# Attention into a hard-swish MLP on one core: a new order and a new sharing of engines, with score tiles as single steps

## The chip, the core and the metric

The kernel runs on one core of a Trainium2 chip. A core has a matrix engine, TensorE (PE in the profile, its weight loads PEld), VectorE (DVE), ScalarE (ACT), GpSimd (POOL) and SyncE (SP), which here only issues DMAs. Each engine takes its instructions in the order in which the program gives them. The metric is the device time of one execution in microseconds (us), the median of three runs.

## The reference

Eight batches of twelve heads with 448 rows of 64 go through attention, and the result through a two-layer MLP whose middle is a hard swish:

```python
q_n, k_n = rmsnorm(q, g_q), rmsnorm(k, g_k)        # x / sqrt(mean(x*x) + 1e-6) * g
scores = 1/sqrt(64) * q_n @ k_n.T                  # per batch and head, 448 x 448
attn = exp(scores - max); attn = attn / (sum + 1e-9)
x = (attn @ v), heads side by side                 # 3584 x 768
h = x @ w_in                                       # 768 x 2048
g = h * clip(h + 3, 0, 6) / 6
out = g @ w_out                                    # 2048 x 768
```

All inputs and the output are fp32.

## The kernel before, in words

Two heads make a pair P, 0 to 47; six pairs make a batch b. The 448 rows of a head are cut into four tiles t of 112. The functions of the kernel do not emit instructions at once. Each calls `plan.add` with the engines that could do the step (`ways`), what it reads and writes, and a function that emits it. A step's number is its place among these calls. The table `WAY` then picks for a step another of its ways than the first, and the list `ORDER` gives the order in which all steps are emitted; since each engine works through its own steps in that order, the list is the program's schedule. The costs, due times, `load` and `since` in the calls served the search that wrote the two tables. They emit nothing.

The stages of a pair are these, with their lines in the profile:

- `load`: q, k and v of the pair by SP (L388), three DMAs of 256 KB each. The rings hold five pairs, so a load waits until the pair five before it has been used.
- `prep`: squares of q and k, on ACT (L401) or POOL (L403); sums over 64 on DVE (L410); the inverse root by Ln and Exp on ACT (L415, L418); the scaling of q and k on POOL (L427; pair 0 on DVE); and the cast of v to bf16 with a column of ones, `va`, on POOL (L351), ACT (L347) or DVE (L345).
- `trans`: q and k turned, into T. Pairs 0 to 12 by PE (L479) with a copy of each half on DVE (L349, L490) or ACT (L347, L488), the k half times the gains. Pairs 13 on by a transposing DMA on SP (L455), and then a scaling of the k half on DVE or ACT (L464). Pairs 8 to 12 turn in the first bank of the two score buffers S. The ring of T holds four pairs.
- `score`: two matmuls for each tile, one for each head, on half the rows of PE each (L510), and an exp on ACT (L519). A tile goes into one of two score buffers S, taken in turn, or, late in the kernel, into X. For pairs 0 to 5 a step is one tile, for 6 to 23 it is two, and for 24 on it is three, two and three tiles for each two pairs. A step of several tiles is emitted as a whole and writes all its buffers.
- `av`: eight matmuls for each tile (L531), summed in the one buffer X over the pair's four tiles.
- `finish`: reciprocal and product on DVE (L547, L550), giving xn; then turned into xT, by PE with a copy for batches 0 and 1 (L566, copies L349 and L347), by a transposing DMA on SP after that (L557).

The MLP takes a batch once its six xT are there. `h_group` b.f makes 128 of the 2048 columns of h for a batch: six matmuls (L587) into one of two buffers M, Relu on ACT (L594) and min and product on DVE (L597). `y_group` takes two batches at a time and 128 rows: twice 16 matmuls of 384 columns (L618), a copy on ACT or DVE and DMAs out (L639). The weights come as four slices of w_in and four of w_out, 768 KB in SBUF each (1.57 MB in fp32), by POOL's DMA queue (L653, L658); h group f needs slice f // 4, and the part p of a y group needs slice p of w_out.

Where PE would idle at the beginning, it runs matmuls on zeros (L356, L536).

Of the kernel before, what the change touches and what calls it, by code (L numbers as in the profile page):

```python
# [14 lines left out]
EXP = mybir.ActivationFunctionType.Exp  # L15
# [6 lines left out]
WAY = {53: 1, 63: 2, 67: 1, 68: 1, 69: 1, 78: 1, 83: 1, 84: 1, 95: 1, 101: 1, 126: 1, 132: 2, 157: 1,  # L22
# [10 lines left out]


class Plan:

# [12 lines left out]
    def add(self, ways, want, fn, reads=(), writes=(), load=(), since=0.0, soon=()):  # L49
        i = len(self.ops)  # L50
        self.way[i] = WAY.get(i, 0)
        eng, occ, fin = ways[self.way[i]]
        soon = dict(soon)
        preds = {}

        def after(p, lat):
            preds[p] = max(preds.get(p, 0.0), lat)

        for r in reads:
            if r in self.last:  # L60
                after(*self.last[r])
            self.readers.setdefault(r, []).append((i, fin))
        for w in writes:
            for p in self.readers.get(w, ()):
                if p[0] != i:
                    after(*p)
            if w in self.last:
                after(*self.last[w])
        for w in writes:
            self.last[w] = (i, soon.get(w, fin))  # L70
            self.readers[w] = []
        self.ops.append((eng, occ, fin, want, fn, preds, load, since))
        self.ways.append(ways)
        return i

    def emit(self, order):

        place = {i: n for n, i in enumerate(order)}
        assert len(place) == len(self.ops)
        for i, o in enumerate(self.ops):  # L80
            assert all(place[p] < place[i] for p in o[5])
        for i in order:
            self.ops[i][4](self.ops[i][0])
# [124 lines left out]
def kernel(  # L208
# [17 lines left out]
    T = 4  # L226
# [110 lines left out]
    def pool(n, rate):  # L337
        return POOL, 0.02 + n * rate, 0.05 + n * rate
# [443 lines left out]
```

## Time and profile before

| | us |
|---|---|
| median of 3 runs | 430.36 (429.74 to 430.75) |
| span of the profiled execution | 427.8 |
| PE busy | 415.1 (97%) |
| ACT busy | 296.7 (69%) |
| DVE busy | 219.6 (51%) |
| POOL busy | 171.1 (40%) |
| first exp / last exp of pair 5 starts | 11.53 / 38.24 |
| first h matmul (L587) | 38.14 |
| first y matmul (L618) | 71.78 |
| last matmul ends | 424.4 |

For the profiled execution no time of its own is given beside its span; the median of the timed runs lies 2.56 us above that span. Shares of busy time are means over a beginning, in which attention for the first batch and the DMAs are all there is to do, and a long middle in which attention and MLP go side by side. So the profile is read by stretches of time. The granted TensorE clock is 1.00 in every stretch.

### The profile page before, as it was taken

The page shows a single profiled execution, that of the slowest core. Times are in us where ns is not written, and L with a number is a line of the kernel's source. Part 1 is how long each engine was busy: PE and PEld are TensorE (multiplying, and loading weights), DVE is VectorE, ACT ScalarE, POOL GpSimd, SP SyncE. Part 2 cuts the span into 40 slices and gives each one's busy share as a digit, 9 for nine tenths or more (in the row PEclk, how much of TensorE's full clock was granted, in tenths as well). Part 3 has the DMA queues.
Part 4 walks back from the last instruction along what each step waited for, and adds up shares of the span by engine and source line. Part 5 has one row for each costly group of instructions (what it writes and reads, how often), then busy time and mean ns, then how long its engine had stood idle before and what let it go on. Part 6 is the DMA issues. An engine that isn't in the chain of part 4 may idle for free.

```text
span 427.8 us, 9914 instructions
## 1 busy us (share of the span) xinstructions
PE 415.1 (97%) x3946; PEld 238.6 (56%) x3946; DVE 219.6 (51%) x405; ACT 296.7 (69%) x535; POOL 171.1 (40%) x188
## 2 busy tenths in 40 slices
PE   9678999999999999999999999999999999999996
PEld 8455455555555555555555555555555555655554
DVE  5665776547787965665545454434434332243211
ACT  5999898889998988968757977575575556222221
POOL 2899865874767866255524340312200000000000
PEclk9999999999999999999999999999999999999999
DMA  8999999698799999668565865352413221021113
GB/s 258 349 249 288 242 240 250 149 267 231 197 237 262 229 234 227 187 155 233 136 170 132 215 156 124 75 125 55 93 33 70 50 60 49 11 75 37 38 38 113
DMA packets 98931, 67.77 MB, mean 158 GB/s; under 512 B 53156, under 2 KB 95428, under 8 KB 98884
## 3 DMA queue, kind: packets, MB, share of 16 engines
q1 hardware_dynamic: 93248, 60.50, 54.5%
q0 software_dynamic: 5248, 6.29, 8.4%
q8 instruction: 31, 0.51, 0.5%
q10 hardware_dynamic: 388, 0.34, 0.3%
q14 instruction: 16, 0.13, 0.1%
HBM read 50.23 MB, written 11.01 MB: 143 GB/s over the span
## 4 chain that ended last, share of the span: by engine, by line
PE 90%; ACT 4%; issue 2%; DVE 1%; DMA 1%; POOL 1%; SPq 0%; POOLq 0%
PE M L587 32%; PE M L618 29%; PE X L531 10%; PE S L510 8%; PE S L618 5%; ACT eT L519 2%; PE X L587 1%; DMA qk<-in_k_dram 1%; PE S L587 1%; PE X L510 1%; PE X L618 1%; POOL qks L427 1%; DVE gT L597 0%; SPq L388 0%; ACT ts L594 0%
## 5 line engine op out<-in xcount | busy, mean ns | idle before, releaser
L519 ACT ACTIVATE eT<-S 112x896 bf16<-112x896 f32 x168 | 148.1, 918 | 13.8 <-PE S L510 13.3
L587 PE MATMUL M<-xT,w_in_sb 128*128 128x448 bf16 x714 | 153.2, 353 | 0.8 <-ACT xT L347 0.4
L618 PE MATMUL M<-w_out_sb,gT 128*128 128x384 bf16 x752 | 135.9, 326 | 0.0
L597 DVE SCALAR_TENSOR_TENSOR gT<-ts,M 128x448 bf16<-128x448 f32 x119 | 73.4, 619 | 101.9 <-ACT ts L594 101.7
L427 POOL TENSOR_TENSOR qks<-qk,rs 112x512 bf16<-112x512 f32 x94 | 96.2, 1043 | 65.5 <-DMA T<-qks 31.9
L618 PEld LDWEIGHTS <-gT 128*128 128x128 bf16 x912 | 84.8, 98 | 61.9 <-issue 9.7
L594 ACT ACTIVATE ts<-M 128x448 f32<-128x448 f32 x119 | 64.8, 548 | 61.0 <-PE M L587 59.8
L587 PEld LDWEIGHTS <-w_in_sb 128*128 128x128 bf16 x768 | 69.9, 98 | 65.7 <-issue 10.9
L403 POOL TENSOR_TENSOR sq<-qk 112x512 f32<-112x512 f32 x56 | 57.7, 1041 | 43.4 <-DMA qk<-in_k_dram 18.2
L531 PEld LDWEIGHTS <-eT 112*128 112x128 bf16 x1536 | 57.1, 97 | 18.1 <-issue 8.2
L410 DVE TENSOR_REDUCE ssq<-sq 112x16 f32<-112x1024 f32 (+1 forms) x50 | 57.9, 1172 | 15.8 <-ACT sq L401 11.9
L531 PE MATMUL X<-va,eT 112*128 112x65 bf16 x1536 | 62.3, 194 | 1.0 <-DVE xT L349 0.8
L510 PE MATMUL S<-T 64*128 64x448 bf16 x336 | 47.3, 354 | 2.1 <-ACT eT L519 1.5
L550 DVE TENSOR_TENSOR xn<-X,rd 112x512 bf16<-112x512 f32 x48 | 33.2, 691 | 1.6
L351 POOL CAST va<-vf 112x512 bf16<-112x512 f32 x20 | 12.3, 613 | 41.1 <-PE X L531 38.8
L510 PEld LDWEIGHTS <-T 64*128 64x128 bf16 x384 | 12.8, 94 | 27.9 <-issue 21.0
L401 ACT ACTIVATE sq<-qk 112x512 f32<-112x512 f32 x40 | 24.9, 629 | 4.7 <-DMA qk<-in_q_dram 2.3
L347 ACT COPY y<-M 128x384 f32<-128x384 f32 x26 | 12.5, 481 | 18.4 <-PE M L618 18.1
L547 DVE RECIPROCAL rd<-X 112x8 f32<-112x8 f32 x48 | 9.8, 204 | 28.1 <-PE X L531 27.9
L349 DVE COPY y<-M 128x384 f32<-128x384 f32 x21 | 11.7, 555 | 22.8 <-PE M L618 22.6
L519 ACT ACTIVATE eT<-X 112x896 bf16<-112x896 f32 x24 | 22.1, 923 | 0.0
L618 PE MATMUL S<-w_out_sb,gT 128*128 128x384 bf16 (+1 forms) x128 | 21.8, 316 | 0.0
(58 smaller groups left out, 188.3 us busy)
## 6 DMA issues: line engine op xcount, KB each, us to landing
qk<-in_q_dram SPq DMA_DIRECT2D x47, 256.0 KB, 4.2
qk<-in_k_dram SPq DMA_DIRECT2D x47, 256.0 KB, 4.0
vf<-in_v_dram SPq DMA_DIRECT2D x47, 256.0 KB, 4.8
w_in_sb<-in_moe_w_in_dram POOLq DMA_DIRECT2D x4, 768.0 KB, 12.7
w_out_sb<-in_moe_w_out_dram POOLq DMA_DIRECT2D x4, 768.0 KB, 14.5
out_dram<-y SPq DMA_DIRECT2D x7, 336.0 KB, 2.8
out_dram<-y SPq DMA_DIRECT2D x8, 288.0 KB, 2.7
out_dram<-y SPq DMA_DIRECT2D x8, 240.0 KB, 3.4
```

Source lines behind the costliest of these rows:

```text
L401: em(nc.scalar.square(out=sq[:, i], in_=x))
L403: em(nc.gpsimd.tensor_tensor(out=sq[:, i], in0=x, in1=x, op=A_MULT))
L410: em(nc.vector.tensor_reduce(out=ssq[:, s].rearrange("p i n -> p (i n)"), in_=sq[:, s].rearrange("p i (n d) -> p (i n) d", d=D), axis=AX_X ...
L427: em((nc.vector if e == DVE else nc.gpsimd).tensor_tensor(out=qks[:, i].rearrange("p t h d -> p h t d"), in0=qk[:, i].rearrange("p h (t d) ...
L510: em(nc.tensor.matmul(out=ps[:, a, 0:S], lhsT=qkT[r, S + t * TP:S + t * TP + 128], rhs=qkT[r, 0:S], start=True, stop=True))
L519: em(nc.scalar.activation(out=eT[:, t, 0:S2].rearrange("p (a s) -> p a s", a=2), in_=ps[0:TP, :, 0:S], func=EXP, bias=0.0, scale=1.0))
L531: em(nc.tensor.matmul(out=X_ps[:, a, i * E1:(i + 1) * E1], lhsT=eT[:, t, c:c + 128], rhs=va[:, a, t, :], start=(t == 0 and i == 0), stop=( ...
L550: em(nc.vector.tensor_tensor(out=xn[:].rearrange("p i a d -> p a i d"), in0=xv[:, :, :, 0:D], in1=rd[:].unsqueeze(3).to_broadcast([TP, 2, ...
L587: em(nc.tensor.matmul(out=ps[:, 0:S], lhsT=w_in_sb[:, kt, f * 128:(f + 1) * 128], rhs=xT[:, kt, :], start=(kt == 0), stop=(kt == NKT - 1)))
L594: em(nc.scalar.activation(out=ts[:], in_=ps[:, 0:S], func=RELU, bias=0.5, scale=1.0 / 6.0))
L597: em(nc.vector.scalar_tensor_tensor(out=gT[:, f, e * S:(e + 1) * S], in0=ts[:], scalar=1.0, in1=ps[:, 0:S], op0=A_MIN, op1=A_MULT))
L618: em(nc.tensor.matmul(out=ps[:, 0:nc0], lhsT=gT[:, f, i * 128:(i + 1) * 128], rhs=w_out_sb[:, f, c0:c0 + nc0], start=(f == 0), stop=(f == ...
```

## The change

The score steps of several tiles are gone: `score` makes one step for each tile. This adds 96 steps, so all numbers behind the first of them shift, and both tables are written anew, by a search over four copies of a model with durations stretched at random. The figures of that model were changed as well (`load`, `since`, some durations, the fields of a step); none of these emits an instruction. No instruction's shape or amount of data is changed.

What the new tables say, counted per engine:

| | before | after |
|---|---|---|
| squares on ACT / POOL | 40 / 56 | 44 / 52 |
| casts of v on ACT / POOL / DVE | 12 / 20 / 16 | 8 / 24 / 16 |
| copies of T (PE's transposes) on ACT / DVE | 10 / 16 | 4 / 22 |
| scalings of T's k half on ACT / DVE | 16 / 19 | 15 / 20 |
| copies of xT on ACT / DVE | 4 / 8 | 2 / 10 |
| copies of y on ACT / DVE | 32 / 25 | 30 / 27 |
| order of the weights on POOL's queue (i: w_in, o: w_out) | i1 i0 o2 i2 i3 o1 o0 o3 | i0 i1 i2 o0 i3 o1 o2 o3 |
| first loads on SP's queue (pair and tensor) | 0q 0k 2q 1v 1k 1q 3v 0v | 0q 0k 1q 2q 2k 1k 3q 3k |

ACT's queue from the first exp to pair 5's last one, in short (E pair.tile: exp; sq: square; n: Ln and Exp of a norm, named where the second of the two stands; cT, cX, va: copies and the cast):

```
before: E0.1 E0.0 E0.3 n2 sq3.k E0.2 E1.1 va2 E1.0 E1.3 E1.2 n3 sq5.k E2.1 E2.0 sq4.q E2.3 E2.2 sq6.q n4 E3.0 E3.1 n5
        E3.2 E3.3 n6 cX2 E4.1 E4.0 E4.3 sq8.q cT6.q E5.1 E4.2 n7 E5.3 cT6.k E5.0 cX4 E5.2
after:  E0.0 E0.1 E0.2 E0.3 sq4.q E1.0 n3 E1.1 n4 E1.2 E1.3 sq6.q n5 sq6.k E2.0 E2.1 E2.2 n6 sq7.q E2.3 E3.0 E3.1 E3.2
        E3.3 E4.0 E4.1 n7 E4.2 E4.3 E5.0 n8 E5.1 E5.2 E5.3
```

The diff, without most of the two tables:

```diff
-WAY = {53: 1, 63: 2, 67: 1, 68: 1, 69: 1, 78: 1, 83: 1, 84: 1, 95: 1, 101: 1, 126: 1, 132: 2, 157: 1,
...
+WAY = {
+    63: 2, 65: 1, 68: 1, 69: 1, 78: 2, 84: 1, 90: 1, 94: 1, 95: 1, 101: 2, 126: 1, 132: 2, 163: 1, 218: 1,
...
-    def add(self, ways, want, fn, reads=(), writes=(), load=(), since=0.0, soon=()):
+    def add(self, ways, want, fn, reads=(), writes=(), load=(), since=0.0, half=False):
...
 ORDER = [
-    8, 9, 20, 13, 21, 22, 15, 23, 11, 24, 28, 10, 25, 19, 29, 53, 26, 12, 30, 27, 14, 54, 31, 16, 55, 32, 33,
...
-            plan.add([(SP, 0.5, 2.5)], want, fn, writes=res, load=(0.84, 60))
+            plan.add([(SP, 0.5, 2.5)], want, fn, writes=res, load=(0.745,))
...
-            plan.add([(SP, 0.6, 2.5)], want, f_d, reads, [(tn, i) for i in range(2)],
-                     load=(1.7, 30))
+            plan.add([(SP, 1.22, 2.5)], want, f_d, reads, [(tn, i) for i in range(2)],
+                     load=(1.25,))
...
-    def score(slots, want):
-        parts = [(P, t, *((X_ps, ("X",)) if wide else sbank())) for P, t, wide in slots]
+    def score(P, t, wide, want):
+        ps, res = (X_ps, ("X",)) if wide else sbank()
+        qkT, eT, n = T_r[P % NT], eT_r[P % NE], P % NE
 
         def f_s(_):
-            for P, t, ps, _ in parts:
-                qkT = T_r[P % NT]
-                for a in range(2):
-                    r = slice(a * 64, a * 64 + 64)
-                    em(nc.tensor.matmul(
-                        out=ps[:, a, 0:S], lhsT=qkT[r, S + t * TP:S + t * TP + 128], rhs=qkT[r, 0:S],
-                        start=True, stop=True))
...
-        plan.add(pe(0.2 + 0.19 * len(parts)), want, f_s, sorted(reads), [p[3] for p in parts], soon=soon)
...
+            for a in range(2):
+                r = slice(a * 64, a * 64 + 64)
+                em(nc.tensor.matmul(
+                    out=ps[:, a, 0:S], lhsT=qkT[r, S + t * TP:S + t * TP + 128], rhs=qkT[r, 0:S],
+                    start=True, stop=True))
...
+        plan.add(pe(0.196), want, f_s, [(("T", P % NT), i) for i in range(2)], [res], half=True)
+        plan.add([act(S2)], want, f_e, [res], [("e", n, t)])
...
-            plan.add([(POOL, 0.8, 3.0)], -20.0, f_i, [], [("w_in", c)], load=(4.56, 95), since=AT_IN[c])
+            plan.add([(POOL, 0.8, 3.0)], -20.0, f_i, [], [("w_in", c)], load=(4.0,), since=AT_IN[c])
...
-            score(slots, gw)
+            for slot in slots:
+                score(*slot, gw)
```

More of the change, by code (lines that the diff above doesn't have):

```diff
@@ L21 @@
 PE, ACT, DVE, POOL, SP = "PE", "ACT", "DVE", "POOL", "SP"
-WAY = {53: 1, 63: 2, 67: 1, 68: 1, 69: 1, 78: 1, 83: 1, 84: 1, 95: 1, 101: 1, 126: 1, 132: 2, 157: 1,
[10 rows of a table removed]
+WAY = {
[11 rows of a table added]
+}
 class Plan:
@@ L52, in add @@
         eng, occ, fin = ways[self.way[i]]
[L53 to L57, printed above, removed]
+        preds = set()
         for r in reads:
             if r in self.last:
-                after(*self.last[r])
-            self.readers.setdefault(r, []).append((i, fin))
+                preds.add(self.last[r])
+            self.readers.setdefault(r, []).append(i)
         for w in writes:
-            for p in self.readers.get(w, ()):
-                if p[0] != i:
-                    after(*p)
+            preds.update(p for p in self.readers.get(w, ()) if p != i)
             if w in self.last:
-                after(*self.last[w])
+                preds.add(self.last[w])
         for w in writes:
-            self.last[w] = (i, soon.get(w, fin))
+            self.last[w] = i
             self.readers[w] = []
-        self.ops.append((eng, occ, fin, want, fn, preds, load, since))
+        self.ops.append((eng, occ, fin, want, fn, preds, load, since, half))
         self.ways.append(ways)
@@ L371, in f_gp @@
             em(nc.vector.tensor_copy(out=gp_t[:], in_=X_ps[:, 0, 0:1]))
-        plan.add([(DVE, 0.15, 0.25)], want, f_g8, [], [("g8",)], since=2.5)
+        plan.add([(DVE, 0.15, 0.25)], want, f_g8, [], [("g8",)], since=3.4)
         plan.add(pe(0.3), want, f_gm, [("g8",)], [("X",)])
@@ L431, in f_sc @@
                     op=A_MULT))
-            plan.add([(DVE, 0.75, 0.85) if P == 0 else pool(n, 1.95e-3)], want + 0.01, f_sc,
+            plan.add([(DVE, 1.0, 1.1) if P == 0 else pool(n, 1.95e-3)], want + 0.01, f_sc,
                      [("qk", P % NQK, i), ("rs", P % NRS, i)], [("qks", P % NQS, i)])
@@ L437, in prep @@
         ways = [(POOL, 0.57, 0.62), act(n, 0.03)][::-1 if P in V_ACT else 1]
-        plan.add(ways + [(DVE, 0.62, 0.7)], want + 2.0, f_v,
+        plan.add(ways + [(DVE, 0.7, 0.8)], want + 2.0, f_v,
                  [("vf", P % NV)], [("va", P % NVA)])
@@ L466, in f_kt @@
                     em(nc.vector.tensor_scalar(x, x, gp_t[:], None, A_MULT, A_ADD, accum_out=junk_t[:]))
-            plan.add([(DVE, 0.62, 0.7), act(S, 0.1)], want + 3.0, f_kt, [("gp",)], [(tn, 1)])
+            plan.add([(DVE, 0.7, 0.8), act(S, 0.1)], want + 3.0, f_kt, [("gp",)], [(tn, 1)])
             return
@@ L500, in sbank, with f_e @@
         return S_r[u], ("S", u)
-    def score(slots, want):
-        parts = [(P, t, *((X_ps, ("X",)) if wide else sbank())) for P, t, wide in slots]
+    def score(P, t, wide, want):
+        ps, res = (X_ps, ("X",)) if wide else sbank()
+        qkT, eT, n = T_r[P % NT], eT_r[P % NE], P % NE
         def f_s(_):
-            for P, t, ps, _ in parts:
-                qkT = T_r[P % NT]
-                for a in range(2):
-                    r = slice(a * 64, a * 64 + 64)
-                    em(nc.tensor.matmul(
-                        out=ps[:, a, 0:S], lhsT=qkT[r, S + t * TP:S + t * TP + 128], rhs=qkT[r, 0:S],
-                        start=True, stop=True))
-        soon = [(p[3], 0.1 + 0.19 * (n + 1) + MM_FIN) for n, p in enumerate(parts)]
-        reads = {(("T", p[0] % NT), i) for p in parts for i in range(2)}
-        plan.add(pe(0.2 + 0.19 * len(parts)), want, f_s, sorted(reads), [p[3] for p in parts], soon=soon)
-        for P, t, ps, res in parts:
-            eT, n = eT_r[P % NE], P % NE
-            def f_e(_, t=t, ps=ps, eT=eT):
-                em(nc.scalar.activation(
-                    out=eT[:, t, 0:S2].rearrange("p (a s) -> p a s", a=2),
-                    in_=ps[0:TP, :, 0:S], func=EXP, bias=0.0, scale=1.0))
-            plan.add([act(S2)], want, f_e, [res], [("e", n, t)])
+            for a in range(2):
[3 more added lines that the diff above has]
+                    start=True, stop=True))
+        def f_e(_):
+            em(nc.scalar.activation(
+                out=eT[:, t, 0:S2].rearrange("p (a s) -> p a s", a=2),
+                in_=ps[0:TP, :, 0:S], func=EXP, bias=0.0, scale=1.0))
+        plan.add(pe(0.196), want, f_s, [(("T", P % NT), i) for i in range(2)], [res], half=True)
+        plan.add([act(S2)], want, f_e, [res], [("e", n, t)])
     def av(P, t, want):
@@ L538, in f_av @@
                     skip_group_check=True))
-        plan.add(pe(0.238), want, f_av, [("e", P % NE, t), ("va", P % NVA)], [("X",)])
+        plan.add(pe(0.246), want, f_av, [("e", P % NE, t), ("va", P % NVA)], [("X",)])
     def finish(P, want):
@@ L559, in f_d @@
                     in_=xn[:].rearrange("p i a d -> p (i a d)")))
-            plan.add([(SP, 0.6, 2.5)], want, f_d, [("xn", P % NXN)], [("xT", b % NXT, j)], load=(0.85, 30))
+            plan.add([(SP, 1.22, 2.5)], want, f_d, [("xn", P % NXN)], [("xT", b % NXT, j)], load=(0.62,))
             return
@@ L589, in f_h @@
                         rhs=xT[:, kt, :], start=(kt == 0), stop=(kt == NKT - 1)))
-            plan.add(pe(0.189 * len(kts)), want + part * dt * 2 / np, f_h,
+            plan.add(pe(0.1897 * len(kts)), want + part * dt * 2 / np, f_h,
                      [("xT", b % NXT, kt) for kt in kts] + [("w_in", f // 4)], [res])
@@ L621, in f_y @@
                             start=(f == 0), stop=(f == NFT - 1)))
-                plan.add(pe(4 * (0.003 + nc0 / 2400)), want + (n * 4 + part) * dt, f_y,
+                plan.add(pe(4 * (0.0033 + nc0 / 2400)), want + (n * 4 + part) * dt, f_y,
                          [("g", g % 2, e, f) for e in es for f in range(part * 4, part * 4 + 4)]
@@ L643, in y_group @@
                 else:
-                    plan.add([(SP, 0.4, 2.4)], want + 8 * dt, f_o,
+                    plan.add([(SP, 0.52, 2.4)], want + 8 * dt, f_o,
                              [("y", yk, n)] if final else [("y", yk, i) for i in range(3)], [],
-                             load=(m * nc0 * 1.4e-5, 110))
+                             load=(m * nc0 * 1.4e-5,))
                 c += m
@@ L660, in f_o @@
                     in_=moe_w_out[c * 512:(c + 1) * 512, :].rearrange("(f p) n -> p f n", p=128)))
-            plan.add([(POOL, 0.8, 3.0)], -20.0, f_o, [], [("w_out", c)], load=(4.8, 150), since=AT_OUT[c])
+            plan.add([(POOL, 0.8, 3.0)], -20.0, f_o, [], [("w_out", c)], load=(4.04,), since=AT_OUT[c])
     H_C, Y_C, A_C = 1.134, 5.216, 2.1
```

259 rows, old and new, of tables (ORDER, WAY) are left out of this document.

## The prediction

> **What bounds the kernel now.** I read the page's engine shares first, then the busy time by stretch, then TensorE's (PE's) waits, and last the queues of the stretch in which PE is not full. The page's busy tenths, 10.7 us to a slice:
>
> ```profile
> PE   9678999999999999999999999999999999999996
> ACT  5999898889998988968757977575575556222221
> POOL 2899865874767866255524340312200000000000
> DMA  8999999698799999668565865352413221021113
> ```
>
> The busy time by stretch (length, then busy us of each engine, granted clock, DMA share, GB/s):
>
> ```profile
> 12.00:16.00 4.00, 2.81 (x45) 1.85 (x46) 2.75 (x4) 3.83 (x8) 4.00 (x5) 1.00 1.09 350
> 25.00:30.00 5.00, 4.18 (x82) 2.76 (x79) 2.77 (x5) 4.97 (x12) 5.00 (x6) 1.00 1.17 258
> 35.00:40.00 5.00, 4.09 (x58) 2.48 (x58) 2.51 (x4) 4.60 (x11) 4.98 (x7) 1.00 1.12 301
> 50.00:55.00 5.00, 5.00 (x45) 2.69 (x44) 4.20 (x10) 4.69 (x11) 3.94 (x4) 1.00 1.17 244
> 100.00:150.00 50.00, 50.00 (x516) 26.65 (x515) 40.06 (x75) 45.37 (x85) 32.80 (x34) 1.00 0.91 228
> ```
>
> From 72 us on, the list of PE's waits is empty: PE is full, and the end is set by how much PE work is left and by when PE fills up. Before about 45 us ACT and POOL are full (4.97 and 5.00 of 5.00) and PE is not. So a new order can save time only ahead of about 72 us, and can lose it anywhere. ACT's own rows between the first exp and the last one of pair 5 (11.5 to 39.2 us; busy us, mean ns, idle before):
>
> ```profile
> L519 ACT ACTIVATE eT<-S 112x896 bf16<-112x896 f32 x24 | 21.0, 915 | 1.0 <-PE S L510 0.9
> L401 ACT ACTIVATE sq<-qk 112x512 f32<-112x512 f32 x6 | 3.8, 628 | 0.0
> L347 ACT COPY xT<-X 128x448 bf16<-128x448 bf16 x2 | 1.1, 546 | 0.0
> L488 ACT ACTIVATE T<-M,gp_t 128x448 bf16<-128x448 bf16 x1 | 0.6, 627 | 0.0
> L347 ACT CAST va<-vf 112x512 bf16<-112x512 f32 x1 | 0.6, 620 | 0.0
> L347 ACT COPY T<-M 128x448 bf16<-128x448 bf16 x1 | 0.5, 523 | 0.0
> ```
>
> Instructions overlap their neighbours by about 0.1 us (a square starts at 22.44, the next exp at 22.96), so one costs the queue its duration less 0.1. Last, PE in order of time: where it first fills up, and what a score run costs.
>
> ```profile
> 43.53 0.54 PE L587 MATMUL M<-xT,w_in_sb 128*128 128x448 bf16 x2 [0.42 <-ACT xT L347]
> 44.49 0.55 PE L510 MATMUL S<-T 64*128 64x448 bf16 x4
> ...
> 143.11 0.42 PE L531 MATMUL X<-va,eT 112*128 112x65 bf16 x8
> 143.36 1.30 PE L587 MATMUL M<-xT,w_in_sb 128*128 128x448 bf16 x6
> 144.50 0.90 PE L531 MATMUL X<-va,eT 112*128 112x65 bf16 x24
> 145.32 0.55 PE L510 MATMUL S<-T 64*128 64x448 bf16 x4
> 145.81 1.48 PE L618 MATMUL M<-w_out_sb,gT 128*128 128x384 bf16 x8
> ```
>
> An attention-times-V step (8 matmuls) takes 143.36 − 143.11 = 0.25; three ahead of a score run take 0.82 where 0.74 is due, so entering a score run costs 0.08 to 0.1. The run of two tiles then takes 0.49 start to start, where runs of three take 0.67: 0.19 a tile and 0.1 besides. One more score run is thus 0.2 us of PE.
>
> **The change, part by part.** No arithmetic is added: the counts of squares, exps, casts, copies and matmuls are equal. Moved are order and engine.
>
> (1) ACT's queue up to pair 5's last exp. Old, behind the first exp at 11.53: 24 exps, 5 squares, 6 Ln and 6 Exp of the norms, one v cast, two T copies, two xT copies; last exp over at 39.16 (38.24 + 0.92). New: 24 exps, 4 squares, the same 12 small ones, no cast, no copy. Gone: one square 0.53, one cast 0.52, xT copies 2 x 0.45, T copies 0.52 and 0.42, in all 2.9. Ahead of the first exp the new queue holds one square more and one cast less. Its chain runs: the fifth load landed at 7.78 (2.78 + 4.99) and loads land about 0.75 apart (0.256 MB at 350 GB/s), so the sixth, now pair 1's k, lands near 8.4; its square until 9.5; the sum on DVE waits for pair 2's (1.2) and takes 0.65, until 10.3; T copy 10.7; scores; first exp near 11.2, 0.35 earlier. With the same 1.4 us of gaps, pair 5's last exp ends at 39.16 − 2.9 − 0.35 = 35.9. **−3.3.** The six instructions go to DVE and POOL. DVE's summed work up to pair 5's xn grows from 25.2 to 29.2 us, with 33 us to do it in; POOL's up to pair 5's last scaling falls from 20 to 18. Neither comes to the front, so the shift itself costs nothing; without that room it would cost its 4 us.
>
> (2) Score tiles singly. In the old order pair 6's tiles 2 and 3 are one step, behind both T8 transposes (in the same banks) and behind an xT copy on ACT; it starts at 44.49, 5.3 after pair 5's last exp. By then the old PE has 21.8 us of its real work behind it. In the new order, tile 2 goes once its own bank is free. After 35.9 come a square 0.53, exp 0.84, exp 0.84, two small ones 0.25, a wait of about 0.4 for the T8 copy, then exp; PE reaches the same amount of work 4 us after pair 5's last exp. 5.3 − 4.0 = 1.3, and 0.3 more because it stands at 22.1 by then. **−1.6**
>
> (3) Score runs. Counted in the order, neighbours in PE's queue taken together: 88 runs before (8, 56 and 24 of one, two and three tiles), 93 after (17, 53, 23). 5 x 0.2 = **+1.0**, on the path since nearly all come where PE is full. If the extra ones all lay in PE's early gaps it would be 0.
>
> (4) Weights. On POOL's queue the first slice of w_in is now first of the eight, seventeenth in its queue (fourteenth before, with slice 1 in front). 12 squares and scalings at 1.0 and one cast at 0.6, started near 10.3, another cast and one wait of 1: issue near 24. PE wants it at about 33.5, ahead of pair 5's last score tile. The issues seen landed after 11.2 to 15.3: 35.2 to 39.3, a wait of 1.7 to 5.8. The lower end is none: the row nearest is slice 1 of the old kernel (issued 17.82, landed 29.0, nothing ahead of it in its queue), and eight loads went out beside it at 0.75 each; now SP waits for POOL's scalings, and about five go out between 22.5 and 31. 11.2 − 3 x 0.75 = 9.0: lands at 33. I take **+0.5**. Slice 1 now is issued at about 32 instead of 17.8 and wanted at 44 (11.2 gives 43.2: no wait; 15.3 gives 3.3); slices 2 and 3 and w_out are wanted 9 to 20 after their issue, and w_out part 3 leaves POOL at about 56 where it left at 61.9.
> [...]
>
> (5) DVE beside POOL. Pair 0's two scalings stay on DVE; they took 1.11 (beside a POOL cast) and 0.68 (alone). Now the second meets POOL's square of pair 2. Bounds 0 and +1.04 (the square); I take the rows' difference, **+0.4**, as it lies on the chain to the first exp.
> [...]
>
> (6) SP's queue. Pair 14's transpose stands at place 45 (55 before), behind it four q and k loads and one more, then pair 13's transpose, and only then pair 12's v load (52; was 36). SP is blocked until pair 14 is scaled and pair 10's scores have freed its T buffer, about 71. The v load then lands near 80 and is wanted by PE near 85; pair 13's T is there near 79 and wanted near 83. Cost 0 to 4 (each of POOL's steps ahead 15% slower); taken **0**, the cover being 4 us.
>
> (7) Later. The PE work between a tile's scores and its use by V has median 7.1 us after the change and 4.3 before, between a full bank and its next use 2.3 and 2.2, between a y group and the next use of its bank 1.6 and 1.4, the least 0.77 and 0.9. Where the old list shows no wait I take **+0.5** for shorter least gaps, between 0 and 3 (the five least gaps each 0.2 short, and one transpose 2 late). The cost figures edited in the plan emit no instruction.
>
> Sum: −3.3 − 1.6 + 1.0 + 0.5 + 0.4 + 0.5 = −2.5. The profiled span is 427.8, so 425.3 after; the median of the runs shown is 430.36, 2.56 above that span, and I carry this over: **427.9**. This case's own range is 426.4 to 429.3.
>
> **The rivals.**
> More is kept: parts 4, 5 and 7 cost nothing and the extra runs fall in gaps: −4.9 + 0.2, 425.7. For it: the freer steps of 7, and POOL's lower sum. Against: DMA's share above 1.0 all the way to 70 us.
> Late weights (the other side): w_in slice 0 takes 15.3 instead of 9, and PE stands from 33.5 to 39.3 in front of pair 5's last tile, ACT dry behind it. 5.8 − 0.5 = +5.3 on the forecast, less some 1.2 that ACT's backlog makes good: 432.0. It decides from 12.5 between issue and landing on (3.0 of wait, of which 0.5 is in the sum, eat the gain). For it: two of the three early w_in rows are at 12.1 and 15.3. Against: fewer loads beside it.
> SP's block: T13 or va12 comes 4 to 6 us late, after PE has filled up, and nothing makes it good: 432. For it: a queue in order with five loads behind a wait. Against: the covers of 4 us.
> Nothing moves: ACT's shorter queue only uncovers DMA, whose 65 us of early transfers (44 loads at 0.75, 8 slices at 4) end near 70 either way: PE fills when it did, and the runs cost 1.0, half of it in gaps: 430.9.
>
> **How the numbers follow.** Forecast 0.48; more kept 0.14; late weights 0.18; SP's block 0.12; nothing moves 0.08. Measuring cannot tell under 0.2% (0.86 us) from no change. Faster: 0.48 + 0.14 and 0.03 of the late-weights cases under 2.6 us of wait, 0.65. Same: 0.02 of late weights, 0.02 of SP's block, 0.04 of nothing moves, 0.08. Slower: the other 0.27. The range, 425.4 to 432.0, leaves out some 0.06 below (the better part of more-is-kept) and 0.14 above (the worse halves of late weights and SP's block).
>
> **What would show it.** Part 1: pair 5's last exp over near 36, DVE and POOL not full between 12 and 36. Part 2: exp of pair 6's tile 2 near 39 instead of 45, and the first L618 matmul near 68 instead of 71.78. Part 3: runs of two score matmuls in the full stretch, 0.2 dearer in all. Part 4: no wait over 1 us on w_in before an L587 matmul. Parts 6 and 7: no PE wait behind 72. I am wrong if PE stands at L587 between 33 and 50, if POOL or DMA and not ACT sets the exps, or if PE's waits behind 72 sum to over 2.

## The result and the profile after

The kernel after takes 431.84 us (median of 19, 430.27 to 435.81), the kernel before 430.62 (19, 429.50 to 432.56): a ratio of 1.0039, 95% interval 1.0020 to 1.0058. It is slower by 0.4%; 427.9 and faster was forecast. The profiled execution of after has a span of 429.5 us, 1.7 above that of before, and a time of 431.26. The h matmul is L578 now (L587 before), the y matmul L609, the score L504, V L522, the scaling L422, the square on POOL L398.

The busy tenths of the page, 10.7 us to a slice:

```profile
PE   7889998999999999999999999999999999999996
ACT  6988987779888778767877784686866564124110
POOL 2999946477754454327131523341604000000000
DMA  8899997888966998575967287724850720131015
```

Busy time by stretch (length, then busy us of PE, PEld, DVE, ACT, POOL, granted clock, DMA share, GB/s), the stretches shown of before and four more:

```profile
12.00:16.00 4.00, 3.84 (x54) 2.79 (x52) 3.06 (x8) 3.79 (x7) 4.00 (x5) 1.00 1.01 335
25.00:30.00 5.00, 4.18 (x74) 2.79 (x71) 4.12 (x10) 4.74 (x8) 4.98 (x6) 1.00 1.01 207
35.00:40.00 5.00, 5.00 (x77) 3.25 (x75) 3.63 (x7) 4.94 (x8) 4.55 (x6) 1.00 1.13 245
50.00:55.00 5.00, 5.00 (x52) 2.69 (x51) 3.32 (x8) 4.69 (x12) 4.44 (x5) 1.00 1.19 205
60.00:70.00 10.00, 9.79 (x93) 5.08 (x91) 6.44 (x14) 8.43 (x15) 2.16 (x3) 1.00 1.15 232
70.00:80.00 10.00, 9.04 (x110) 5.14 (x111) 4.41 (x8) 7.02 (x14) 7.52 (x9) 1.00 0.46 109
110.00:125.00 15.00, 14.22 (x163) 7.55 (x160) 10.70 (x22) 11.99 (x24) 10.18 (x12) 1.00 0.89 183
125.00:160.00 35.00, 34.38 (x307) 18.69 (x305) 19.20 (x34) 29.07 (x52) 15.83 (x17) 1.00 0.92 218
```

PE is full between 35 and 40 us, where it had 4.09 of 5.00. So the beginning did become shorter. But PE is short again later: by 1.2 us between 60 and 80 us, where the old one was short by 0.45, and by 1.4 between 110 and 160 us, where the old one was full. POOL has 2.16 of 10 us to do from 60 to 70. PE's waits behind 45 us, after (the tile and line that waited, who ended the wait; us in all, times, longest):

```profile
PE M L578 <- DVE gT L588: 1.0, 2, 0.7
PE X L522 <- POOL va L346: 0.6, 1, 0.6
PE M L609 <- DVE gT L588: 0.4, 1, 0.4
PE M L578 <- ACT y L342: 0.2, 1, 0.2
```

**PE's lag** makes this countable: the wall time less the PE work done by then, each step of PE's order taken at its price in the rows (a matmul of h 0.190, four matmuls of y 0.65, a step of V 0.246, four transposes 0.2, scores 0.19 a tile and 0.2 a run; the last eight steps of y have half the columns and half the price). Where PE is full the lag stands still. PE's whole work is 400.8 us before and 401.6 after. The lag in us at:

| run | 40 | 60 | 80 | 150 | 400 | span |
|---|---|---|---|---|---|---|
| before | 21.7 | 22.9 | 23.9 | 23.8 | 23.5 | 427.8 |
| after | 19.5 | 19.7 | 21.7 | 23.6 | 23.6 | 429.5 |

After was ahead by 3.2 us at 60 us. By 160 us (23.9) it had lost all of it. The list of waits above shows only 2.2 us of this: start to start, a wait costs PE some 0.17 more than its row says (at 116.48 the list has 0.71 and the lag grows by 0.88), and gaps below 0.15 us are not listed. The 1.7 of the span are 0.8 more PE work, 0.2 of lag, and 0.7 behind PE's end.

The first loss, in the timeline of SP, POOL, DVE and PE, after (start, us, what; in brackets the idle time ahead of it and who ended it):

```profile
53.61 0.93 SPq L383 DMA_DIRECT2D qk<-in_k_dram  x2
74.91 1.35 SPq L450 DMA_TRANSPOSE T<-qks  x1
76.32 0.57 SPq L383 DMA_DIRECT2D qk<-in_q_dram  x1
...
66.16 1.03 POOL L398 TENSOR_TENSOR sq<-qk 112x512 f32<-112x512 f32 x1 [7.99 <-DMA qk<-in_k_dram]
68.87 1.04 POOL L398 TENSOR_TENSOR sq<-qk 112x512 f32<-112x512 f32 x1 [1.68 <-DMA qk<-in_k_dram]
69.86 0.61 POOL L346 CAST va<-vf 112x512 bf16<-112x512 f32 x1
...
71.50 1.22 DVE L405 TENSOR_REDUCE ssq<-sq 112x16 f32<-112x1024 f32 x1 [0.33 <-POOL sq L398]
72.63 0.61 DVE L588 SCALAR_TENSOR_TENSOR gT<-ts,M 128x448 bf16<-128x448 f32 x1
...
70.52 0.64 PE L522 MATMUL X<-va,eT 112*128 112x65 bf16 x16 [0.58 <-POOL va L346]
73.30 0.81 PE L609 MATMUL M<-w_out_sb,gT 128*128 128x384 bf16 x4 [0.40 <-DVE gT L588]
```

Pair 14's and 15's loads go out at 52.6 to 54.5 us, into a DMA that also carries weight slices, three at first and four from 57.4 to 59.2 us. The k loads issued at 53.61 and 54.07 land at 65.99 and 68.74, 12.4 and 14.7 us later. POOL stands 8 us in front of pair 15's square (66.16), and behind it, in POOL's order, stands pair 10's cast, whose data had been there since 45.1 us at the latest: PE waits for it at 70.52. The squares' sums on DVE are late with them, and stand ahead of the MLP's product (72.63): PE waits at 73.30. SP issues nothing from 54.5 to 74.91, because pair 14's transpose waits. The second loss is of the same kind:

```profile
115.20 0.68 DVE L461 TENSOR_SCALAR_CACHE_REDUCE T<-T,gp_t 128x448 bf16<-128x448 bf16 x1 [1.84 <-DMA T<-qks]
115.81 0.62 DVE L588 SCALAR_TENSOR_TENSOR gT<-ts,M 128x448 bf16<-128x448 f32 x1
...
116.48 1.29 PE L578 MATMUL M<-xT,w_in_sb 128*128 128x448 bf16 x6 [0.71 <-DVE gT L588]
```

DVE waits for pair 18's transpose, which is not urgent, and the product that PE needs stands behind it.

The 0.7 behind PE's end are the last outputs. SP issues its last one 0.5 us behind PE's last matmul (before 0.4), and it lands 2.3 us later (before 1.7), with eight outputs issued from 423.63 us on, where before had four from 423.92 on.

```profile
423.63 2.50 SPq L630 DMA_DIRECT2D out_dram<-y  x5
425.82 0.38 ACTq L630 DMA_DIRECT2D out_dram<-y  x1
```

### The profile page after: what moved, and what is told of

The parts are those of the page before. It is cut to its first block, busy times and chain, and to the rows that moved or that the text cites. A ratio compares the mean times of both kernels' runs of the same rounds, so it can differ in the third digit from the quotient of the medians.

```text
span 429.5 us, 9863 instructions
## 1 busy us (share of the span) xinstructions
PE 416.8 (97%) x3946; PEld 240.6 (56%) x3946; DVE 220.8 (51%) x417; ACT 290.7 (68%) x524; POOL 168.8 (39%) x188
## 4 chain that ended last, share of the span: by engine, by line
PE 74%; DMA 4%; DVE 1%; POOL 1%; issue 1%; ACT 1%; SPq 0%; ACTq 0%; POOLq 0%
PE M L609 27%; PE M L578 25%; PE X L522 7%; PE S L504 6%; PE S L609 5%; DMA T<-qks 2%; PE X L504 1%; PE X L578 1%; DMA vf<-in_v_dram 1%; PE S L578 1%; DMA qk<-in_q_dram 1%; DVE ssq L405 1%; POOL sq L398 1%; PE X L609 1%; DVE gT L588 1%
## 5 line engine op out<-in xcount | busy, mean ns | idle before, releaser
L578 PE MATMUL M<-xT,w_in_sb 128*128 128x448 bf16 x714 | 157.4, 353 | 1.3 <-DVE gT L588 1.0
L609 PE MATMUL M<-w_out_sb,gT 128*128 128x384 bf16 x752 | 138.3, 326 | 0.5 <-DVE gT L588 0.4
L422 POOL TENSOR_TENSOR qks<-qk,rs 112x512 bf16<-112x512 f32 x94 | 96.5, 1042 | 103.3 <-ACT rs L413 65.5
L609 PEld LDWEIGHTS <-gT 128*128 128x128 bf16 x912 | 84.8, 98 | 61.9 <-issue 9.7
L578 PEld LDWEIGHTS <-w_in_sb 128*128 128x128 bf16 x768 | 68.8, 98 | 64.8 <-issue 13.3
L398 POOL TENSOR_TENSOR sq<-qk 112x512 f32<-112x512 f32 x52 | 53.6, 1040 | 51.5 <-DMA qk<-in_q_dram 17.8
L522 PEld LDWEIGHTS <-eT 112*128 112x128 bf16 x1536 | 60.4, 97 | 20.9 <-issue 7.1
L522 PE MATMUL X<-va,eT 112*128 112x65 bf16 x1536 | 65.8, 194 | 1.3 <-DVE xT L344 0.7
L504 PE MATMUL S<-T 64*128 64x448 bf16 x336 | 49.3, 354 | 1.8 <-ACT eT L509 1.3
L396 ACT ACTIVATE sq<-qk 112x512 f32<-112x512 f32 x44 | 27.4, 633 | 7.0 <-DMA qk<-in_k_dram 3.1
L504 PEld LDWEIGHTS <-T 64*128 64x128 bf16 x384 | 13.7, 94 | 27.0 <-issue 19.3
L342 ACT COPY y<-M 128x384 f32<-128x384 f32 x25 | 12.0, 479 | 20.6 <-PE M L609 16.0
L609 PE MATMUL S<-w_out_sb,gT 128*128 128x384 bf16 (+1 forms) x128 | 22.6, 316 | 0.0
L346 POOL CAST va<-vf 112x512 bf16<-112x512 f32 x24 | 14.5, 612 | 8.7 <-ACT rs L413 6.1
## 6 DMA issues: line engine op xcount, KB each, us to landing
w_out_sb<-in_moe_w_out_dram POOLq DMA_DIRECT2D x4, 768.0 KB, 15.1
```

Of the source, the lines that this page charges most:

```text
L396: em(nc.scalar.square(out=sq[:, i], in_=x))
L398: em(nc.gpsimd.tensor_tensor(out=sq[:, i], in0=x, in1=x, op=A_MULT))
L422: em((nc.vector if e == DVE else nc.gpsimd).tensor_tensor(out=qks[:, i].rearrange("p t h d -> p h t d"), in0=qk[:, i].rearrange("p h (t d) ...
L504: em(nc.tensor.matmul(out=ps[:, a, 0:S], lhsT=qkT[r, S + t * TP:S + t * TP + 128], rhs=qkT[r, 0:S], start=True, stop=True))
L522: em(nc.tensor.matmul(out=X_ps[:, a, i * E1:(i + 1) * E1], lhsT=eT[:, t, c:c + 128], rhs=va[:, a, t, :], start=(t == 0 and i == 0), stop=( ...
L578: em(nc.tensor.matmul(out=ps[:, 0:S], lhsT=w_in_sb[:, kt, f * 128:(f + 1) * 128], rhs=xT[:, kt, :], start=(kt == 0), stop=(kt == NKT - 1)))
```

## The experiments

Three theories stood at first. In-order: steps that wait for a DMA stand ahead of urgent ones in the queues of ACT, DVE and POOL, and moving them mends it. Supply: between 57 and 160 us loads land too late, whatever stands first. Score runs: the extra runs cost the time. In the edits, 14q is a load, dT a transpose by DMA, sq a square, va a cast of v, kt a scaling of T's k half, R a Relu, G the product behind it, E an exp, S a score tile, wi and wo weight slices. The kernels of the experiments have the h matmul in L577, those with fillers in L586. "Before" is measured beside each group.

**Four first runs.**

```diff
 e1_pair14, against after
- SP:   13k 15q 14q 15k 14k dT14
+ SP:   13k 14q 14k 15q 15k dT14
- POOL: wo3 sq15k sq14k va10 sq15q
+ POOL: wo3 sq14k va10 sq15k sq15q
 e2_late, against after
- SP:   dX13 23q 23v 20v 23k dT18
+ SP:   dX13 dT18 23q 23v 20v 23k
  ACT:  va21 moved behind R2.4, kt24 behind E21.1, sq28q behind R2.9
 e3_both: both
 e4_joined: after's order up to the fifth h group (44 us), before's order and engines from there
```

> The changed kernel with pair 14's q and k loads put ahead of pair 15's on SP's queue, and pair 14's square and pair 10's v cast put ahead of pair 15's square on POOL's queue; nothing else. In-order theory (the early gain is lost where a step that is not urgent waits for a DMA in front of one that is): the three steps of PE's lag near 66, 70.5 and 74 us (0.3, 0.75, 0.75) go, so 1.5 to 1.8 us less than the changed kernel, a ratio to the kernel before near 1.000. Supply theory (DMA and POOL deliver too little between 57 and 160 us, whatever stands first): the wait moves to pair 11 or 12, and the time stays within 0.5 us of the changed kernel's, ratio near 1.004. Score-run theory (the loss is PE's own, the five extra score runs): no change, 1.004.

> The changed kernel with four moves later on: pair 18's transposing DMA ahead of three loads on SP's queue, and on ACT pair 21's v cast, pair 24's k scaling and pair 28's square each put behind the Relu or exp that they stood ahead of. In-order theory: the steps of PE's lag near 117, 123, 137, 140 and 153 us (0.9, 0.2, 0.5, 0.2, 0.2) go, 1.5 to 2.0 us less than the changed kernel, ratio near 0.9995. Supply theory: the same waits come back a few us later, less than 0.5 us gained. Score-run theory: no change, 1.004.

> Both sets of moves. In-order theory: 3.0 to 3.8 us less than the changed kernel, ratio near 0.996, so faster than the kernel before by some 1.7 us, with PE's lag behind its own work near 20 us to the end instead of 23.9. Supply theory: with the first hole mended the second grows, ratio 1.002 or more. Score-run theory: 1.004.

> The changed kernel's order and engines up to the first four h groups of batch 0 (about 44 us), and from there the order and engines of the kernel before for all that is left (the last four weight slices in the order w_in 3, w_out 1, 2, 3). In-order theory: the early gain of 3.2 us is kept, since the later order of the kernel before has no step on ACT or DVE that waits for a DMA in front of an urgent one, and the late runs of score tiles are the old ones: 427.2 to 428.2, ratio near 0.993 to 0.995. Supply theory: the old later order, now begun 3 us sooner, finds its loads and weights not there and stalls for as long: ratio near 1.000. Score-run theory: the old runs come back from 44 us on, 0.6 of the loss, but nothing of the early gain is lost either; ratio 0.993.

| run | median | ratio to before (431.00), 95% | lag 40 | 60 | 80 | 150 | 400 |
|---|---|---|---|---|---|---|---|
| e1_pair14 | 432.15 | 1.0038 (1.0015 to 1.0061) | 20.6 | 20.8 | 21.5 | 23.8 | 24.2 |
| e2_late | 430.94 | 0.9998 (0.9981 to 1.0016) | 20.6 | 20.8 | 23.2 | 24.3 | 24.3 |
| e3_both | 430.19 | 0.9984 (0.9962 to 1.0005) | 21.8 | 22.0 | 22.8 | 23.9 | 23.9 |
| e4_joined | 435.08 | 1.0094 (1.0075 to 1.0113) | 21.0 | 22.8 | 28.9 | 29.1 | 28.7 |

Each move mended its own place: e1 lost 0.7 between 60 and 80 us (after 2.0), e2 1.1 between 80 and 150 (after 1.9), and e3 1.9 between 60 and 150 (after 3.9). But the lag at 150 us came out at 24 all the same: e1 and e2 lost the rest in the other stretch, and e3's profile had begun 2.3 us later. In the median e3 lies 1.7 us below after (2.4 by the ratios), where in-order had 3.0 to 3.8, so the moves alone did not decide between the theories. e4, which was to keep the gain (427.2 to 428.2), failed in another way. Among its waits of PE:

```profile
PE M L577 <- DMA w_in_sb<-in_moe_w_in_dram: 3.7, 1, 3.7
```

The old order wants slice 3 of w_in sooner than the joined queue brings it (issued at 47.80, landed at 65.58; in before it was issued at 43.01 and landed at 56.25). Behind this wait PE's granted clock stands at 0.50 from 66.3 to 69.7 us, so not all of the 6.1 us that the lag grows between 60 and 80 us is the slice's.

**SP, the score runs, the start.**

```diff
 e5_sp: e1_pair14 and
- SP:   15k dT14 16q 17k 16k 17q 18q dT13 12v 18k 14v 13v
+ SP:   15k 16q 17k 16k 17q 12v 14v 13v dT14 18q dT13 18k
 e6_sp_late: e5_sp and the moves of e2_late
 e7_split_runs, against before, 20 times from pair 24 to 38
- PE:   S24.0 S24.1 S24.2 Y0.5
+ PE:   S24.0 S24.1 Y0.5 S24.2
 e8_warm, against after: four groups of zero matmuls ahead of the gains' matmul
```

> The edits of e1_pair14, and on SP's queue pair 14's transpose is moved behind seven loads that stood behind it (16.q, 17.k, 16.k, 17.q, 12.v, 14.v, 13.v). Supply theory, in the form that SP's 20 us behind that transpose (54.5 to 74.9, nothing issued) start the shortage: these loads are issued before 63 us, POOL's squares and casts of pairs 12 to 17 have their data by 80, PE's lag at 150 us falls from 23.8 to 21 to 22, the time to 429.5 to 430.5. In-order theory: the loads were not what PE waited for; lag at 150 us 23.5 to 24, 431.5 to 432.5. A third way: the loads meet the weight slices in the DMA engines, a slice lands later, PE waits for it at L608 or L577 by 1 us or more, 433.

> e5_sp and the later moves of e2_late together. If the supply from 54 to 75 us and the steps standing in front of urgent ones behind 100 us each cost what they seem to, lag at 150 us is 21 to 21.5 and the time 429.0 to 429.8, below e3_both (430.2) and below the kernel before. If the lag is set by something that neither touches, 430.2 as e3_both or above.

> The kernel before, with the last tile of 20 score runs of pairs 24 to 38 emitted behind the PE step that followed the run: 108 runs in place of 88, nothing else. Score-run theory (0.2 us for each run): 4 us more, 434.5 to 435. If a run costs nothing of its own: 430.6. If only the later exp matters, an amount without relation to the number of runs, with PE waits behind ACT.

> The kernel after, with four groups of zero matmuls moved ahead of the gains' matmul, as the kernel before has them. If PE's wait of 1.6 us for the gains at 2 to 3.6 us is what makes the start later in some executions, that wait is gone, the first score stands at 10.6 to 11.2, and the median falls by 0.3 to 1 us, to 430.9 to 431.5, with the slowest executions gone. If the first score waits for the loads and the norm alone, nothing moves: 431.8.

| run | median | ratio to before (430.91), 95% | lag 40 | 60 | 80 | 150 | 400 |
|---|---|---|---|---|---|---|---|
| e5_sp | 431.43 | 1.0013 (0.9987 to 1.0038) | 19.9 | 20.1 | 21.3 | 22.9 | 23.0 |
| e6_sp_late | 430.58 | 1.0004 (0.9980 to 1.0029) | 22.0 | 22.6 | 24.0 | 25.4 | 25.3 |
| e7_split_runs | 435.45 | 1.0109 (1.0081 to 1.0136) | 23.1 | 24.5 | 25.4 | 25.4 | 25.4 |
| e8_warm | 432.55 | 1.0021 (0.9997 to 1.0046) | 20.9 | 21.1 | 22.9 | 24.7 | 25.4 |

e7 settles the price of a run: 20 more take 4.5 us, and with 0.2 a run in PE's work (404.8 against 400.8) the lag stands at 25.4 from 80 to 400 us, so 0.2 is right. Why a run costs it, no run here shows. With five runs more, it makes 1 us at most of what went wrong. e5: the loads went out earlier and the lag at 150 us fell by 0.9 against e1, but now slice 3 of w_out came late (0.8 us at L608): with the loads out earlier, the w_out slices landed 18.6 us after their issue in the median (16.3 in e1). e6 was not the better version that it was expected to be (429.0 to 429.8). e8 took PE's wait for the gains away, but its first score then waited 1.5 us for the copy of T and stood at 11.56 (after 11.21); the median is no lower.

In e6 the start itself was late, and the busy time by stretch shows why (the granted clock is third from the right):

```profile
18.00:20.00 2.00, 1.18 (x18) 0.58 (x14) 2.00 (x5) 1.67 (x4) 2.00 (x4) 1.00 0.66 194
20.00:22.00 2.00, 1.38 (x27) 0.99 (x25) 0.96 (x4) 1.97 (x6) 2.00 (x3) 0.99 0.75 229
22.00:24.00 2.00, 2.00 (x39) 1.91 (x35) 0.99 (x2) 1.39 (x3) 1.94 (x3) 0.50 1.07 338
24.00:26.00 2.00, 1.62 (x13) 0.91 (x14) 1.97 (x6) 1.42 (x3) 1.98 (x3) 0.50 0.90 260
26.00:28.00 2.00, 2.00 (x24) 1.36 (x21) 1.44 (x2) 1.74 (x3) 2.00 (x3) 0.50 0.77 221
28.00:30.00 2.00, 2.00 (x39) 1.64 (x37) 0.50 (x2) 0.59 (x2) 2.00 (x3) 0.80 0.90 132
```

PE is busy for 1.18 and 1.38 of 2.00, and then its clock is halved for 6.8 us. The profiles of e3, e4, e7 and e8 show a halved clock between 20 and 29 us too, those of before, after, e1, e2 and e5 do not.

**Supply and clock.**

```diff
 e9_half_loads, against after
+                n = 1 if 14 <= P < 26 else 2
-                em(nc.sync.dma_start(out=dst, in_=rows))
+                em(nc.sync.dma_start(out=dst[:, 0:n], in_=rows[:, 0:n]))
 e10_fill (against after), e11_fill_both (e3_both), e12_fill_sp_late (e6_sp_late): steps of
+            for _ in range(n):
+                em(nc.tensor.matmul(
+                    out=M_r[0][:, S:512], lhsT=zero_t[:], rhs=zero_t[:, 0:512 - S], start=False, stop=True,
+                    skip_group_check=True))
```

> The kernel after, but the 36 loads of q, k and v of pairs 14 to 25 bring one head of the two (128 KB in place of 256; the other head's half of the buffer keeps an older pair's data, so the output of these pairs is wrong). Order, engines and every other instruction as they are. Supply theory: what PE loses between 60 and 160 us is data that arrive late, so most of it goes: PE's lag at 150 us is 21.5 or less in place of 23.6, the time 429.5 to 430. If the order of the steps alone makes the waits, they stand where they were: 23.5 to 24, 431.8.

> The kernel after, with 76 more zero matmuls of 64 columns (0.03 us each) on PE in the five gaps between 18 and 28.4 us: 24 ahead of pair 2's tile 0, 6, 12 and 20 and 14 behind it. Clock theory: in half of the profiled executions so far the granted clock stands at 0.50 for 3 to 7 us between 20 and 28 us, because PE stood still too much just before; filled, it stays at 1.00, PE's lag at 40 us stays at 19.5 to 20.5 (up to 22 with the dip), and the median falls from 431.8 by 0.5 to 1 us, the slowest executions by 2. If the gaps have nothing to do with the dip: 431.8 with the same scatter, or up to 1 more for what the fillers delay.

> e3_both with the fillers of e10_fill. Clock theory: 429.5 to 429.9 with little scatter, below the kernel before; otherwise 430.2 or more.

> e6_sp_late with the fillers of e10_fill. Clock theory: its executions at full clock had 429.9, so the median falls from 430.6 to 429.3 to 429.9; the lag at 150 us is 22 to 23. Otherwise 430.6.

| run | median | ratio to before (430.49), 95% | lag 40 | 60 | 80 | 150 | 400 |
|---|---|---|---|---|---|---|---|
| e9_half_loads | 429.59 | 0.9964 (0.9942 to 0.9986) | 20.1 | 20.3 | 20.4 | 20.4 | 20.8 |
| e10_fill | 432.07 | 1.0031 (1.0010 to 1.0051) | 20.3 | 20.5 | 23.0 | 24.1 | 24.4 |
| e11_fill_both | 429.54 | 0.9967 (0.9949 to 0.9985) | 20.3 | 20.6 | 21.8 | 21.8 | 22.3 |
| e12_fill_sp_late | 430.60 | 0.9987 (0.9966 to 1.0008) | 20.8 | 21.0 | 21.6 | 21.8 | 23.5 |

e9 is the run that decides. With after's order untouched, and only less to load, PE's lag stays at 20.4 to beyond 150 us. All of its PE waits from 45 to 430 us:

```profile
core 0 of [0], span 426.4 us
PE X L505 <- DVE xn L542: 0.2, 1, 0.2
```

And from the timelines of SP and POOL:

```profile
54.13 0.85 SPq L384 DMA_DIRECT2D qk<-in_k_dram  x2
74.42 1.35 SPq L451 DMA_TRANSPOSE T<-qks  x1
...
64.49 2.03 POOL L399 TENSOR_TENSOR sq<-qk 112x512 f32<-112x512 f32 x2 [5.74 <-DMA qk<-in_k_dram]
66.47 0.60 POOL L346 CAST va<-vf 112x512 bf16<-112x512 f32 x1
```

SP stands as long as in after (to 74.42), so its standing still alone costs nothing. The two halved k loads issued last ahead of the transpose, at 54.13 and 54.55, land after 7.7 and 9.9 us, and pair 10's cast comes at 66.47 in place of 69.86, ahead of its use. Behind 80 us the engines hardly wait for a DMA any more. What POOL, ACT and DVE stood waiting for DMAs between 80 and 160 us, summed over the lists of waits, in us:

| | POOL | ACT | DVE |
|---|---|---|---|
| before | 0.3 | 0 | 0 |
| after | 15.5 | 2.4 | 1.8 |
| e9_half_loads | 3.3 | 0 | 0 |

The clock is not the reason: at full clock (a mean of 0.997 or more) e9 has 428.43 (six of ten executions), and e10, after with the fillers, 432.07 beside it. Without late data there is no loss.

The fillers keep the clock: in the 72 executions of the six kernels that have them the mean granted clock is never below 0.997; of the 133 of before that stood beside the experiments, 52 are below. What they are worth in time is not clear: the ratio to before falls by 0.0008 (e10 against after), 0.0017 (e11 against e3) and 0.0017 (e12 against e6), all within the intervals, and only e11 came to the median that was expected.

**What is left to the order.** Two more kernels on the filled base, and the fillers on before.

```diff
 e13_slice_first: e11_fill_both and
- POOL: sc9k wo0 sq12k wi3 wo1
+ POOL: sc9k wi3 wo0 sq12k wo1
 e14_before_fill: before, 92 filler matmuls in the four gaps between 15 and 24.8 us
 e15_two_more: e13_slice_first and
- ACT:  E40.3 sq47q R5.9 E41.1
+ ACT:  E40.3 R5.9 E41.1 sq47q
- DVE:  rd36 red42 cY xn36 G5.1
+ DVE:  rd36 cY xn36 G5.1 red42
```

> e11_fill_both with w_in slice 3 issued on POOL's queue ahead of w_out slice 0, 2 us sooner. If PE's wait of 1.1 us for that slice at 64 us is lost time, it goes, and the time falls from 429.5 to 428.5 to 429; if what starts sooner is then late at 115 us as in the kernels before (PE's lag at 150 us comes back to 22 to 23), 429.5; if slice 0 of w_out is now late at L617, 430.

> The kernel before with 92 zero matmuls of 64 columns in its four gaps between 15 and 24.8 us. Clock theory: no execution with a lower clock is left, the median is that of the executions of before at full clock, 430.1 in place of 430.5 to 431.0; then 0.5 of the 1 us of e11_fill_both is the filler's and the rest the order's. If it is 429.5 or less, all of it is the filler's; if it is 430.9 or more, the fillers delay as much as they save.

> e13_slice_first with two steps that wait for data put behind the MLP step that stood behind them: on ACT pair 47's square of q behind pair 41's second exp (it held the Relu of batch 5's group 9 by 1.75 us at 300 us), on DVE pair 42's sums behind the product of batch 5's group 1 (0.58 us at 272 us). In-order theory: the lag's two steps behind 270 us (0.32 and 0.98) go, and the time falls from 429.3 to 428.0 to 428.6. If the data's lateness holds PE whatever stands first, the lag at 400 us stays near 22.2 and the time at 429.3.

| run | median | before | ratio, 95% | lag 40 | 60 | 80 | 150 | 400 |
|---|---|---|---|---|---|---|---|---|
| e13_slice_first | 429.30 | 430.08 | 0.9974 (0.9958 to 0.9990) | 20.6 | 20.8 | 20.9 | 21.2 | 22.2 |
| e14_before_fill | 430.49 | 430.08 | 1.0003 (0.9981 to 1.0025) | 23.2 | 24.6 | 25.5 | 25.5 | 25.2 |
| e15_two_more | 429.10 | 431.01 | 0.9944 (0.9917 to 0.9971) | 20.5 | 20.8 | 20.8 | 21.6 | 21.8 |

With slice 3 of w_in first, PE has no wait listed from 45 to 250 us, and the lag grows by 0.4 between 60 and 150 us in place of after's 3.9; nothing is loaded less. What remained at 300 us was the in-order kind. From ACT's timeline in e13:

```profile
301.52 0.63 ACT L404 ACTIVATE sq<-qk 112x512 f32<-112x512 f32 x1 [1.75 <-DMA qk<-in_q_dram]
302.06 0.53 ACT L593 ACTIVATE ts<-M 128x448 f32<-128x448 f32 x1
```

and PE's wait there, which the list of waits has from 260 to 320 us:

```profile
PE M L586 <- DVE gT L596: 0.8, 1, 0.8
```

A square that waits for its load holds the Relu that PE's next bank needs. Moved behind it (e15), this wait is gone; of the 0.7 to 1.3 us expected, 0.2 came in the median, which does not stand out of the scatter, and two other waits (0.6 and 0.4) stand in the profile. e14 shows that the zero matmuls give before nothing. (Its profiled execution, 0.8 us above its median, began late: the first exp stood at 13.22, ahead of the fillers.) So the order makes the difference of 1.2 us between e13 and e14, measured side by side; against the executions of before at full clock in the same group (median 429.86 of 17) it is 0.6.

So both theories were half of it. Data land late because loads and weights share the DMA (7.7 and 9.9 us in place of 12.4 and 14.7 when the loads are halved); PE pays only where an urgent step stands behind one that waits for them. In e13 POOL, ACT and DVE still wait 13.6 us for DMAs between 80 and 160 us (19.7 in after, by the sums above), and PE waits for none of it. Taking away either cause, the load (e9) or the wrong neighbours and the late slice (e13), leaves PE full up to 250 us, but for 0.2 us in e9. e15 is faster than both kernels. Part of its ratio is the lower clock in many executions of before: against before's executions at full clock (median 430.0 of 81) it gains 0.9 us.

## Why the prediction was wrong

**Parts 1 and 2 (−4.9, with 4 and 5 −4.0)** hold in kind, 0.8 too large. The lag at 60 us is 3.2 smaller. Part 1 alone gave about half: pair 5's last exp is over at 37.6, not 35.9 (39.16 before), 1.6 earlier and not 3.3. The first exp came at 11.63, not 11.2, and exps wait 1.8 us for PE's scores, 0.9 before; 1.4 of it falls behind 31 us, where PE is full and ACT no longer sets the pace alone. Pair 6's tile 2 starts its exp at 40.55 (45.23 before, near 39 forecast), 3.0 behind pair 5's last exp where before it was 6.1. The first y matmul starts at 69.12 (68 forecast).

**Part 3 (+1.0)** is nearly right: PE's work is 0.8 us more (one of the five runs lies among the zero matmuls), and e7 measures the price.

**Part 4 (+0.5)**: w_in slice 0 was issued at 24.1, as said, and PE did not wait for it: 0. That is partly luck: it landed at 35.08, 0.25 us ahead of the first h matmul (35.33), and a PE that wanted it at 33.5, as forecast, would have stood 1.6. The rival's danger is real elsewhere: slice 3 of w_in cost 3.7 us in e4 and 1.1 in e11. And the range of 11.2 to 15.3 was read from slices of w_in alone; two of w_out in before had taken 17.8 and 18.1.

**Part 5 (+0.4)**: 0. Pair 0's second scaling took 0.68 here, from 7.58 us on, when POOL's square was just over (7.47). In e1 it began at 7.41, 0.1 behind the square (7.30 to 8.34), and took 1.48; in e2 and e3 0.95 and 0.82. So the cost in these four profiles, 0 to 0.8 above the 0.68, lay within the bounds.

**Part 6 (0)**: SP stood 20 us, till 74.9 (71 forecast), and I looked only at what stood behind the transpose. By e9 the standing alone cost nothing, by e5 mending it is worth 0.7 us in the median, with intervals that overlap.

**Part 7 (+0.5, between 0 and 3) is the step that failed.** From 60 to 160 us PE lost 4.1 us, and 0.9 in the old order: 3.2 in place of 0.5. I had read from the empty list of waits that PE keeps what it has won, and sized this part by gaps between PE's own steps. But the list was empty because PE came late: with PE 3 us earlier, data that still land when the DMA brings them are 3 us later for it, and POOL's 8 us in front of a load at 66 us hit a cast that PE needed. The sign set for it, waits listed behind 72 us of over 2 in all, did not even show (1.6): the list leaves out part of each wait. Before's own loads issued from 47 to 61 us had taken 9 to 14 us to land, about as after's at 53 and 54 us (11 to 15), and PE had not waited. Of the rivals, "late weights" and "SP's block" had the time (432), which is luck: PE did not wait for slice 0, and by e9 SP's standing alone cost nothing, though late data behind a full PE were the right kind of cause. "Nothing moves" (430.9) had the DMA's early transfers as the limit, with the wrong place: PE did fill early, and lost it again afterwards.

**Behind PE's end** I had no term: 0.7.

**The base.** I added 2.56, from the profiled span to the median. Wherever both are known for one execution they differ by 1.8, so the profiled execution of before had a time of 429.6, 0.8 under the median. The forecast would have been 427.1 for a like execution; this does not explain the miss, it makes it larger.

## What to carry to other kernels

An empty list of waits on the full engine says only that its suppliers keep up with its present lateness. Before counting a gain at the beginning as kept, look up how early each supplier finishes ahead of its use, and which urgent steps stand in order behind one that waits for a DMA. Price a change of order by the steps that stand behind waiting ones, and test it by halving the transfers: if the loss goes, the data are late, and moving two or three steps may do the same.

## What was not expected of the hardware

The granted clock of PE fell to 0.50 between 20 and 29 us in five of the first ten profiles, for 3.4 us (e4, e7, e8) or 6.8 us (e3, e6). In e6 it is 0.50 from 22 to 28 us, and in the 4 us ahead of that PE was busy for 2.56 us. In before PE was busy for 3.02 of the 5 us from 15 to 20, and the clock stayed at 1.00: the busy time ahead of it does not tell by itself whether the clock falls, and what sets a fall these runs do not show. Nor is it fixed by the kernel: of the 133 executions of before beside the experiments 52 have a mean clock below 0.997, with a median of 431.6, and the other 81 have 430.0. With 76 zero matmuls of 64 columns (92 in e14), 0.03 us each, put into the gaps, the mean clock was 0.998 or more in all 72 executions.

A weight slice of 1.57 MB by POOL's queue landed after 9 to 24 us, by what else was in the DMA: 10.3 (median of w_in) and 12.7 (w_out) with the loads halved, 11.0 and 15.1 in after, 11.8 and 19.9 with seven loads moved ahead (e6); the longest, 24.3, is in e4. A load of 256 KB issued at 54 us beside the slices landed 14.7 us later.
